# Mixture-of-experts lists summed in SBUF by matmuls of one-hot place parts, instead of records scattered to memory

## The chip, the cores and the metric

The kernel runs on one core of a Trainium2 chip. The metric is device time in microseconds for one execution, the median of several runs. The profile is of one execution; its times are in microseconds from the start of the span. Engines: PE is the matrix engine (PEld its weight loads), DVE the vector engine, ACT the scalar engine, POOL the GpSimd engine, SP the engine whose queue issues most transfers.

## The reference

Clustered attention on 4 batches x 8 heads x 768 tokens x 64 dimensions, followed by a top-2 mixture of experts on its output (3072 tokens, 512 wide, 8 experts with 1024 hidden units):

```python
mask = q_assign[:, :, :, None] == k_assign[:, :, None, :]   # nearest of 16 centroids
attn = softmax(where(mask, scale * q @ k.T, -1e9)) @ v
...
noisy_logits = x @ w_gate + log1p(exp(x @ w_noise)) * noise
top2 = np.argpartition(-noisy_logits, 2, axis=1)[:, :2]
...
for e in range(E):
    for k in range(2):
        mask = top2[:, k] == e
        h = np.maximum(x[mask] @ w1[e], 0.0)
        out[mask] += top2_w[mask, k, None] * (h @ w2[e])
```

So each token belongs to two experts, with two weights. An expert works on the list of its tokens, and the lists depend on the data.

## The kernel before

**Attention** runs over 16 pairs of heads (four pairs to a batch), 12 steps to a pair, 192 steps in all, in an order of instructions that is fixed by hand: the table `AT` gives for each piece of work the step (in thirds) at which it is issued, and each engine runs its instructions in the order of issue. A step t issues, in this order: the pieces placed at t; `scores(t)` (L477: four matmuls on PE, two exponentials on ACT); `split_p(t - 1)` (L489: the low half `pl` of the exponentials, one subtraction on POOL, L495); pieces placed at t + 1/3; `values(t - 4)` (L498: 18 small matmuls on PE, of which the last six read `pl`, L518); pieces placed at t + 2/3. So PE may run some four steps ahead of POOL. The pieces placed are the preparation of later pairs (transposes and similarities to centroids, `a_...`, the row maxima `b_max`, L446, two matmuls and two reductions on DVE), the values' scaling (`v_...`), and, for each finished batch, the gate.

**The gate** of batch b (`g_logits`, `g_turn`, `g_gate`) works out for 768 tokens the two experts, the two weights, and each token's place in its expert's list: `places` counts by matmuls with a triangle and with ones, `self.base` carries the counts on from batch to batch. A place is a whole number 4096 e + n; its low 7 bits are the partition, the bits above it the tile of 128 places and the expert. Small operations on DVE work in the PSUM tile `aux`, which also holds half of the maxima of `b_max`.

**The lists** are in memory: `tbl` has for each partition, expert and tile a record (token, weight), cleared in `zero_list` to the token number N, which transfers pass over. `g_list` (L697) is called 12 times for each batch, one step apart from step z + 24 on (steps 76, 124 and 172 for the first three batches); each call is a one-element memset on POOL (`spacer`, L700) and an indirect transfer that POOL issues (L701), which scatters 128 records. The last batch's gate and its 12 scatters stand in the experts' stage.

**Experts.** Each expert has room for 832 tokens, six and a half tiles of 128 (T = 7); `extra` (L851) is a branch with loops for longer lists, run only where the counts ask for it. For expert 0 four tiles are taken from the first three batches only (`TA = 4`): their list `lst0` is loaded by `load_list(0)` at step 183, and `gather_x` (L923: a memset and an indirect transfer on POOL) is issued at steps 185 to 188. In `experts` (L731) the last batch's gate is cut into four parts with a block of layer 1 (12 matmuls of 512 columns, L951, then ACT L960 and DVE L961) after each; then come `count` (four small DVE operations), `g_list`, four rounds of splitting a part of w2 (L903 and L904) and a block of layer 1, `load_list(1)` (the whole list from memory), the gathers of tiles 4 to 6, and layer 2 of tiles 0 to 3, with the transposes of tiles 4 to 6 (`turn_x`, L941) ahead of tile 3's. Layer 2 is L990; DVE weighs its rows (L997, L999) and POOL scatters them into `out` (L1003). For experts 1 to 7 the rows of `out` are gathered first (L966).

## Time and profile before

| | us |
|---|---|
| median of 3 runs | 1154.22 (1153.69 to 1156.89) |
| profiled execution: its time / its span | 1154.92 / 1153.1 |
| PE busy | 1076.4 (93%) |
| DVE busy | 596.7 (52%) |
| POOL busy | 589.6 (51%) |
| ACT busy | 480.4 (42%) |
| scatters of records (L701) on POOL | 51.8 in 48 |
| granted PE clock, mean | 0.969 |

Attention ends at about 520 us of the span, and expert 0's layer 2 begins at 552. A row of the timeline is: start, duration, engine, line, operation, output <- inputs, count, and in brackets the idle time before it with what ended it. A row of the stretches is: the stretch, its length, busy time with count for PE, PEld, DVE, ACT and POOL, the granted clock, the share of the transfer engines and GB/s. A row of the groups is: line, engine, operation, shapes, count, busy us, mean ns, and the idle time before with its releasers.

### The profile page before, as it was taken

The numbers are of one execution on the slowest core, as the hardware profiler recorded it, in microseconds if no ns is written. First come the engines' busy times: TensorE is split into PE (matmuls) and PEld (weight loads), VectorE is DVE, ScalarE is ACT, GpSimd is POOL, SyncE is SP. The second block draws the span as 40 slices with busy tenths as digits, with TensorE's granted clock in tenths as the row PEclk, the third lists the DMA queues.
The fourth block names the chain that finished last, engine by engine and source line by source line (L and its number), as shares of the span: only waits on it lengthen the run. The fifth ranks groups of instructions, "written<-read, shape, count | busy, mean of one in ns | idle before, by whom it ended". The sixth has DMA issues, their size and how long they took to land. (4 is left out here: it accounts for less than half of the span.)

```text
span 1153.1 us, 22350 instructions
## 1 busy us (share of the span) xinstructions
PE 1076.4 (93%) x8658; PEld 954.6 (83%) x8658; DVE 596.7 (52%) x1286; ACT 480.4 (42%) x961; POOL 589.6 (51%) x631
## 2 busy tenths in 40 slices
PE   4899899998999899869899999999999999999995
PEld 4588887898888788757799989889898898998984
DVE  5877665876687668436235334433344244433411
ACT  3475656675777566534133303223133132231300
POOL 4776664789578958991645224332343233423311
PEclk8899999999999999969999999999999999999998
DMA  8866776664656444113326225323352244323200
GB/s 224 189 151 152 188 185 194 158 158 110 192 122 159 113 127 122 33 43 118 109 75 210 81 102 166 120 93 109 127 172 73 77 162 129 118 83 131 74 31 31
DMA packets 87678, 144.46 MB, mean 125 GB/s; under 512 B 14296, under 2 KB 65880, under 8 KB 87057
## 3 DMA queue, kind: packets, MB, share of 16 engines
q1 hardware_dynamic: 72272, 106.45, 34.7%
q0 software_dynamic: 13712, 36.42, 9.4%
q8 instruction: 69, 1.13, 0.4%
q10 hardware_dynamic: 1584, 0.13, 0.1%
q14 instruction: 41, 0.33, 0.1%
HBM read 78.21 MB, written 26.53 MB: 91 GB/s over the span
## 5 line engine op out<-in xcount | busy, mean ns | idle before, releaser
L495 POOL TENSOR_TENSOR pl<-pe 128x768 f16<-128x768 f32 x192 | 280.6, 1471 | 97.4 <-ACT pe L486 90.0
L951 PE MATMUL ring<-xT,w1t 128*128 128x416 f32 (+2 forms) x1536 | 290.3, 350 | 0.0
L951 PEld LDWEIGHTS ring<-xT,w1t 128*128 128x128 f32 x1536 | 282.7, 188 | 6.6 <-DVE xT L904 0.3
L990 PE MATMUL ring<-w2t,hT 128*128 128x512 f32 x1152 | 273.7, 394 | 0.0
L990 PEld LDWEIGHTS ring<-w2t,hT 128*128 128x128 f32 x1152 | 214.5, 189 | 43.3
L486 ACT ACTIVATE pe<-ring,l 128x384 f32<-128x384 f32 x384 | 202.9, 578 | 102.5 <-PE ring L485 93.4
L1003 POOL DMA_INDIRECT out<-yo,lst x56 | 65.6, 1172 | 234.7 <-DVE yo L999 187.1
L457 DVE TENSOR_REDUCE aux<-ring 128x1 f32<-128x384 f32 x192 | 107.9, 562 | 94.6 <-PE ring L454 90.2
L485 PE MATMUL ring<-A 128*128 128x384 f32 x384 | 145.4, 379 | 0.0
L485 PE MATMUL ring<-B 128*128 128x384 f32 x384 | 134.3, 350 | 5.0 <-DMA B<-nt 4.9
L960 ACT ACTIVATE hT<-ring 128x416 fp32r<-128x416 f32 (+3 forms) x128 | 56.7, 488 | 180.6 <-PE ring L951 180.5
L961 DVE SCALAR_TENSOR_TENSOR hT<-ring,hT 128x416 fp32r<-128x416 f32 (+3 forms) x128 | 66.2, 553 | 124.0 <-ACT hT L960 123.8
L930 POOL DMA_INDIRECT xg<-xs,lst x56 | 65.5, 1170 | 124.9 <-PE ring L941 105.0
L454 PE MATMUL ring<-A 128*128 128x384 f32 x384 | 114.0, 372 | 14.5 <-DMA A<-mk 8.6
L999 DVE SCALAR_TENSOR_TENSOR yo<-ring,lst,xt 128x512 f32<-128x512 f32 (+1 forms) x49 | 36.7, 750 | 166.6 <-PE ring L990 146.1
L903 ACT ACTIVATE xT<-ring 128x512 fp32r<-128x512 f32 (+1 forms) x56 | 31.0, 565 | 178.0 <-PE ring L941 177.9
L457 DVE TENSOR_REDUCE mm<-ring 128x1 f32<-128x384 f32 x192 | 104.9, 546 | 0.0
L512 PE MATMUL av<-vv,pe 128*128 128x65 f16 x1152 | 100.9, 198 | 0.0
L514 PE MATMUL av<-vv,pe 128*128 128x64 f16 x1152 | 99.9, 196 | 0.0
L454 PEld LDWEIGHTS ring<-A 128*128 128x128 f32 x384 | 71.6, 197 | 31.0 <-ACT pe L486 14.1
L512 PEld LDWEIGHTS <-pe 128*128 128x128 bf16 x1152 | 83.6, 101 | 13.9 <-issue 11.4
L518 PE MATMUL av<-vv,pl 128*128 128x65 f16 x1152 | 68.9, 197 | 20.1 <-POOL spacer L700 12.6
(172 smaller groups left out, 1363.1 us busy)
## 6 DMA issues: line engine op xcount, KB each, us to landing
stg<-in_moe_w SPq DMA_DIRECT2D x64, 512.0 KB
A<-hl SPq DMA_DIRECT2D x30, 384.0 KB
B<-hl SPq DMA_DIRECT2D x30, 384.0 KB
vt<-in_v SPq DMA_DIRECT2D x8, 768.0 KB
out<-zt SPq DMA_DIRECT2D x12, 512.0 KB
xs<-xt SPq DMA_DIRECT2D x4, 1536.0 KB
A<-hl SPq DMA_DIRECT2D x60, 96.0 KB
B<-hl SPq DMA_DIRECT2D x30, 192.0 KB
```

The costliest lines, as they stand in the source:

```text
L454: nc.tensor.matmul(t, A[:, 0, s, j * 128:j * 128 + 128], A[:, 1, s, n * 384:n * 384 + 384], start=True, stop=True)
L457: nc.vector.tensor_reduce(o, t, axis=X, op=OP.max, negate=True)
L485: nc.tensor.matmul(t, M[:, 1 - qi, s, ks], M[:, qi, s, ns], start=not qi, stop=bool(qi))
L486: nc.scalar.activation(pe[:, n], t, AF.Exp, bias=self.l64[:, 0:1], scale=self.scale)
L495: nc.gpsimd.tensor_tensor(lo, pe, hi, op=OP.subtract)
L512: nc.tensor.matmul(av[:, j, :], ph[:, js], vv[:, hh, kj, 64:129], start=(kc == 0 and j == 0), stop=False, skip_group_check=True)
L514: nc.tensor.matmul(av[:, j, :64], ph[:, js], vv[:, hh, kj, 0:64], start=False, stop=False, skip_group_check=True)
L518: nc.tensor.matmul(av[:, j, :], pl[:, js], vv[:, hh, kj, 64:129], start=False, stop=(kc == NJ - 1), skip_group_check=True)
L951: nc.tensor.matmul(p, self.w1t[:, wi, c, f * 128:f * 128 + 128], self.xT[:, xi, c, n0:n1], start=(i == 0), stop=(i == 3 * ND - 1))
L961: nc.vector.scalar_tensor_tensor(h1, x, 0.0, h0, op0=OP.max, op1=OP.subtract)
L990: nc.tensor.matmul(p, self.hT[:, hi, f, t * 128:t * 128 + 128], self.w2t[:, wi, f], start=(i == 0), stop=(i == 3 * NF - 1))
L1003: i = nc.gpsimd.indirect_dma_start(out=self.out, out_offset=bass.IndirectOffsetOnAxis(ap=en[:r, 0:1], axis=0), in_=yo[:r], in_offset=None, ...
```

## The change

- `zero_list` and the 48 scatters are gone from the normal course. The table is cleared and all 48 scatters are issued only inside the branch for lists of more than seven tiles (`table`).
- The gate ends in other operations: the place is cut into its low 7 bits and the rest; `hot` compares the rest of 12 places for each partition with the 56 numbers of expert and tile (one DVE operation of 672 elements, `eq`); ACT copies of the low part, of a weight and of the place are added. It needs the same small DVE operations but one.
- `g_list` is called once for each batch, at step z + 26 (steps 78, 126 and 174, and at its old place in the experts' stage). It works in two halves of six columns: DVE makes `hot` (128 x 6 x 128: the low part compared with 0 to 127), POOL makes `ent` in four products of 128 x 168 (`eq` times token number minus N, and `eq` times weight), and six fp32 matmuls of `hot` (128 x 128) and `ent` (128 x 112) add into one PSUM tile. `hot` and `ent` have one buffer each. DVE then adds the 128 x 112 sum into `lacc` in SBUF, which begins as N for the tokens and 0 for the weights.
- `load_list` copies the token numbers from `lacc` to integers on DVE, in place of the loads from memory. Weights are read from `lacc` (`lsw0` for the first four tiles of expert 0).
- Five constants more are made at the start on POOL, and the values' tile `vv` has two buffers in place of three.

```diff
-    logstep=0.667, turn=7.667, list=24.0, lstep=1.0, bstep=1.0,
+    logstep=0.667, turn=7.667, list=26.0, bstep=1.0,
...
+        self.T = -(-CAP // 128)
+        self.upper = consts.tile([128, E, self.T], F32, name="upper")
+        nc.gpsimd.iota(self.upper, pattern=[[4096, E], [128, self.T]], base=0, channel_multiplier=0,
+                       allow_small_or_imprecise_dtypes=True)
+        self.lower = consts.tile([128, 128], F32, name="lower")
+        nc.gpsimd.iota(self.lower, pattern=[[1, 128]], base=0, channel_multiplier=0,
+                       allow_small_or_imprecise_dtypes=True)
+        self.tokn = consts.tile([128, B, NJ], F32, name="tokn")
+        nc.gpsimd.iota(self.tokn, pattern=[[self.S, B], [1, NJ]], base=-self.N, channel_multiplier=NJ,
+                       allow_small_or_imprecise_dtypes=True)
+        self.lacc = consts.tile([128, 2, E * self.T], F32, name="lacc")
+        nc.gpsimd.memset(self.lacc[:, 0], float(self.N))
+        nc.gpsimd.memset(self.lacc[:, 1], 0.0)
+        self.code = consts.tile([128, B, NJ, 2], I32, name="code")
+        self.wts = consts.tile([128, B, NJ, 2], F32, name="wts")
...
-                for j in range(2 * NJ):
-                    at(z + T["list"] + T["lstep"] * j, self.g_list, b, j)
-        at(T["zero"] - 4, self.zero_list)
+                at(z + T["list"], self.g_list, b)
...
-            vv = self.wk.tile([128, 4, NJ, 130], F16, name="vv", bufs=3)
+            vv = self.wk.tile([128, 4, NJ, 130], F16, name="vv", bufs=2)
...
-        self.recs = []
...
-    def zero_list(self):
-        nc, E = self.nc, self.E
-        ti = self.gp.tile([128, self.ET, 2], I32, name="lg")
-        nc.gpsimd.memset(ti[:, :, 0:1], self.N)
-        nc.gpsimd.memset(ti[:, :, 1:2], 0)
-        W = 2 * self.ET
-        nc.sync.dma_start(rap(self.tbl, 0, [[E * W, 128], [W, E], [1, W]]),
-                          ti.rearrange("p t c -> p (t c)")[:, None, :].to_broadcast([128, E, W]))
...
-        pk = lambda i: T["pk"][:, i]
...
-        pi = lambda i: T["p"][:, 440 + 2 * NJ * i:440 + 2 * NJ * i + 2 * NJ].bitcast(I32).rearrange("p (j k) -> p j k", k=2)
+        pf = lambda i: T["p"][:, 440 + 2 * NJ * i:440 + 2 * NJ * i + 2 * NJ].rearrange("p (j k) -> p j k", k=2)
+        pi = lambda i: pf(i).bitcast(I32)
...
-        rf = lambda: T["rec"].bitcast(F32)
+        wt = lambda k: self.wts[:, b, :, k]
...
-        do(lambda: nc.gpsimd.tensor_copy(T["rec"][:, :, :, 0], self.tok[:, b, :, None].to_broadcast([128, NJ, 2])))
+        do(lambda: v.tensor_scalar(T["lo"], pi(0), 127, None, op0=OP.bitwise_and))
...
-        do(lambda: v.tensor_scalar(pi(1), pi(0), 127, 8, op0=OP.bitwise_and, op1=OP.logical_shift_left))
-        do(lambda: v.tensor_scalar(pk(0), pi(0), 7, None, op0=OP.logical_shift_right))
-        do(lambda: nc.scalar.activation(rf()[:, :, 0, 1], pm(1), AF.Copy))
-        def end():
-            v.tensor_tensor(pk(1), pi(1), pk(0), op=OP.bitwise_or)
-            v.tensor_tensor(rf()[:, :, 1, 1], pm(1), m(1), op=OP.mult)
-            self.addr, self.rec = pk(1), T["rec"]
-        do(end)
+        do(lambda: nc.scalar.activation(pf(1), T["lo"], AF.Copy))
+        do(lambda: v.tensor_tensor(pf(2), pi(0), T["lo"], op=OP.subtract))
+        do(lambda: nc.scalar.activation(wt(0), pm(1), AF.Copy))
+        do(lambda: v.tensor_tensor(wt(1), pm(1), m(1), op=OP.mult))
+        def hot():
+            n, W = 2 * NJ, E * self.T
+            T["eq"] = gp.tile([128, NJ, 2, W], F32, name="lg")
+            v.tensor_tensor(T["eq"].rearrange("p j k w -> p (j k) w"),
+                            pf(2).rearrange("p j k -> p (j k)")[:, :, None].to_broadcast([128, n, W]),
+                            self.upper.rearrange("p e t -> p (e t)")[:, None, :].to_broadcast([128, n, W]), op=OP.is_equal)
+            self.eq, self.low = T["eq"], pf(1).rearrange("p j k -> p (j k)")
+        do(hot)
+        do(lambda: nc.scalar.activation(self.code[:, b], pi(0), AF.Copy))
...
-    def g_list(self, b, i):
-        nc, tc = self.nc, self.tc
-        j, k = divmod(i, 2)
-        nc.gpsimd.memset(self.spacer, 0.0)
-        i = nc.gpsimd.indirect_dma_start(
-            out=self.tbl, out_offset=bass.IndirectOffsetOnAxis(ap=self.addr[:, j, k:k + 1], axis=0),
-            in_=self.rec[:, j, k, :], in_offset=None)
-        for o in self.recs:
-            tc.declare_no_dep(i.ins, o.ins, reason="each place is one token's")
-        self.recs.append(i)
+    def g_list(self, b):
+        nc, NJ, W = self.nc, self.NJ, self.E * self.T
+        t = self.ps()[:, :2 * W]
+        n = NJ // 2
+        for h in range(2):
+            js = slice(n * h, n * h + n)
+            hot = self.gp.tile([128, NJ, 128], F32, name="hot", bufs=1)
+            nc.vector.tensor_tensor(hot, self.low[:, NJ * h:NJ * h + NJ, None].to_broadcast([128, NJ, 128]),
+                                    self.lower[:, None, :].to_broadcast([128, NJ, 128]), op=OP.is_equal)
+            ent = self.gp.tile([128, n, 2, 2, W], F32, name="ent", bufs=1)
+            for k in range(2):
+                nc.gpsimd.tensor_tensor(ent[:, :, k, 0], self.eq[:, js, k],
+                                        self.tokn[:, b, js, None].to_broadcast([128, n, W]), op=OP.mult)
+                nc.gpsimd.tensor_tensor(ent[:, :, k, 1], self.eq[:, js, k],
+                                        self.wts[:, b, js, k, None].to_broadcast([128, n, W]), op=OP.mult)
+            ent = ent.rearrange("p j k a w -> p (j k) (a w)")
+            for i in range(NJ):
+                nc.tensor.matmul(t, hot[:, i], ent[:, i], start=(h == 0 and i == 0), stop=(h == 1 and i == NJ - 1))
+        acc = self.lacc.rearrange("p a w -> p (a w)")
+        nc.vector.tensor_tensor(acc, t, acc, op=OP.add)
+    def table(self):
+        nc, B, NJ, E = self.nc, self.B, self.NJ, self.E
+        ti = self.gp.tile([128, self.ET, 2], I32, name="lg")
+        nc.gpsimd.memset(ti[:, :, 0:1], self.N)
+        nc.gpsimd.memset(ti[:, :, 1:2], 0)
+        W = 2 * self.ET
+        nc.sync.dma_start(rap(self.tbl, 0, [[E * W, 128], [W, E], [1, W]]),
+                          ti.rearrange("p t c -> p (t c)")[:, None, :].to_broadcast([128, E, W]))
+        rec = self.gp.tile([128, B, NJ, 2, 2], I32, name="rec", bufs=1)
+        pk = self.gp.tile([128, 2, B, NJ, 2], I32, name="pk", bufs=1)
+        for k in range(2):
+            nc.gpsimd.tensor_copy(rec[:, :, :, k, 0], self.tok)
+        nc.gpsimd.tensor_copy(rec.bitcast(F32)[:, :, :, :, 1], self.wts)
+        nc.vector.tensor_scalar(pk[:, 0], self.code, 127, 8, op0=OP.bitwise_and, op1=OP.logical_shift_left)
+        nc.vector.tensor_scalar(pk[:, 1], self.code, 7, None, op0=OP.logical_shift_right)
+        nc.vector.tensor_tensor(pk[:, 0], pk[:, 0], pk[:, 1], op=OP.bitwise_or)
+        for b in range(B):
+            for j in range(NJ):
+                for k in range(2):
+                    nc.gpsimd.indirect_dma_start(
+                        out=self.tbl, out_offset=bass.IndirectOffsetOnAxis(ap=pk[:, 0, b, j, k:k + 1], axis=0),
+                        in_=rec[:, b, j, k, :], in_offset=None)
...
-        self.lst0 = self.mw.tile([128, self.TA, 2], I32, name="lst0")
+        self.lst0 = self.mw.tile([128, self.TA], I32, name="lst0")
+        self.lsw0 = self.mw.tile([128, self.TA], F32, name="lsw0")
...
-        W = 2 * self.ET
+        nc, TA = self.nc, self.TA
...
-            assert len(self.recs) == 2 * self.NJ * (self.B - 1)
-            self.nc.sync.dma_start(self.lst0.rearrange("p t c -> p (t c)"), rap(self.tbl, 0, [[self.E * W, 128], [1, 2 * self.TA]]))
+            nc.vector.tensor_copy(self.lst0, self.lacc[:, 0, 0:TA])
+            nc.vector.tensor_copy(self.lsw0, self.lacc[:, 1, 0:TA])
...
-            self.nc.sync.dma_start(self.lst.rearrange("p e t c -> p e (t c)"),
-                                   rap(self.tbl, 0, [[self.E * W, 128], [W, self.E], [1, 2 * self.T]]))
+            nc.vector.tensor_copy(self.lst, self.lacc[:, 0])
...
-        return self.lst0[:, t] if e == 0 and t < self.TA else self.lst[:, e, t]
+        if e == 0 and t < self.TA:
+            return self.lst0[:, t:t + 1]
+        i = e * self.T + t
+        return self.lst[:, i:i + 1]
+    def weight(self, e, t):
+        if e == 0 and t < self.TA:
+            return self.lsw0[:, t:t + 1]
+        i = e * self.T + t
+        return self.lacc[:, 1, i:i + 1]
...
-        for i in range(2 * NJ):
-            self.g_list(b, i)
+        self.g_list(b)
...
+            self.table()
...
-            in_offset=bass.IndirectOffsetOnAxis(ap=self.entry(e, t)[:r, 0:1], axis=0),
+            in_offset=bass.IndirectOffsetOnAxis(ap=self.entry(e, t)[:r], axis=0),
...

```

More of the change, by code (lines that the diff above doesn't have):

```diff
@@ L604, in begin @@
             T["m"] = gp.tile([128, 3, NJ], F32, name="gm", bufs=1)
-            T["rec"] = gp.tile([128, NJ, 2, 2], I32, name="rec", bufs=2)
-            T["pk"] = gp.tile([128, 2, NJ, 2], I32, name="pk", bufs=2)
+            T["lo"] = gp.tile([128, NJ, 2], I32, name="glo", bufs=1)
             T["tmp"] = gp.tile([128, NJ, 2, E], F32, name="gtmp", bufs=1)
@@ L739, in experts @@
         self.w2t = mo.tile([128, 2, NF, DM], F32R, name="w2t")
-        self.lst = mo.tile([128, E, T, 2], I32, name="lst")
+        self.lst = mo.tile([128, E * T], I32, name="lst")
         A = (0, TA * 128)
@@ L967, in gather_out @@
             out=self.pv[t % 6][:r], out_offset=None, in_=self.out,
-            in_offset=bass.IndirectOffsetOnAxis(ap=self.entry(e, t)[:r, 0:1], axis=0),
+            in_offset=bass.IndirectOffsetOnAxis(ap=self.entry(e, t)[:r], axis=0),
             bounds_check=self.N - 1, oob_is_err=False)
@@ L994, in layer2 @@
         en = self.entry(e, t)
-        wt = en.bitcast(F32)[:r, 1:2]
+        wt = self.weight(e, t)[:r]
         if e == 0:
@@ L1003, in layer2 @@
         i = nc.gpsimd.indirect_dma_start(
-            out=self.out, out_offset=bass.IndirectOffsetOnAxis(ap=en[:r, 0:1], axis=0),
+            out=self.out, out_offset=bass.IndirectOffsetOnAxis(ap=en[:r], axis=0),
             in_=yo[:r], in_offset=None, bounds_check=self.N - 1, oob_is_err=False)
@@ L1014, in run @@
         self.CAP, self.TA = CAP, 4
-        self.T = -(-CAP // 128)
         self.CT = CAP // 128 * 128
```

## Prediction

> **What bounds the kernel now.** I read the page first, then the waits of the matrix engine (PE), then the table of stretches, then the timelines of POOL, PE and DVE around the record scatters. From the page:
>
> ```profile
> span 1153.1 us, 22350 instructions
> ...
> PE 1076.4 (93%) x8658; PEld 954.6 (83%) x8658; DVE 596.7 (52%) x1286; ACT 480.4 (42%) x961; POOL 589.6 (51%) x631
> ```
>
> PE is busy for 93% of the span, so matmuls added are paid in full unless they fall into PE's idle time, and each PE wait removed is a gain. The longest total PE waits (waited-for, us in total, times, longest):
>
> ```profile
> PE av L518 <- POOL spacer L700: 12.6, 7, 2.8
> ...
> PE av L518 <- POOL pl L495: 7.3, 7, 2.2
> ...
> PE ring L941 <- DMA xg<-xs,lst: 3.1, 1, 3.1
> ```
>
> The first is what the change can remove: PE waits for `pl`, which stands on POOL behind a scatter (L700 is the spacer ahead of it). The POOL timeline (start, duration) shows how, and rows that later parts use:
>
> ```profile
> 29.28 0.89 POOL L342 TENSOR_TENSOR vv<-vt,vv 128x384 f16<-128x384 f32 x1 [16.04 <-ACT vv L341]
> ...
> 461.67 1.47 POOL L495 TENSOR_TENSOR pl<-pe 128x768 f16<-128x768 f32 x1 [0.23 <-ACT pe L486]
> ...
> 465.10 0.09 POOL L700 MEMSET spacer<- 1x1 f32 x1
> 465.36 1.02 POOL L701 DMA_INDIRECT tbl<-rec,pk  x1 [0.16 <-POOL spacer L700]
> 466.40 1.48 POOL L495 TENSOR_TENSOR pl<-pe 128x768 f16<-128x768 f32 x1
> 467.81 0.09 POOL L700 MEMSET spacer<- 1x1 f32 x1
> ...
> 501.07 0.54 POOL L929 MEMSET xg<- 128x512 f32 x1
> ...
> 504.39 0.53 POOL L929 MEMSET xg<- 128x512 f32 x1
> ...
> 513.01 7.16 POOL L495 TENSOR_TENSOR pl<-pe 128x768 f16<-128x768 f32 x5
> ...
> 543.57 1.02 POOL L701 DMA_INDIRECT tbl<-rec,pk  x1 [23.22 <-issue]
> ...
> 566.33 1.05 POOL L930 DMA_INDIRECT xg<-xs,lst  x1 [5.54 <-DMA lst<-tbl]
> ```
>
> With a scatter in it a step costs POOL 467.81 - 465.10 = 2.71 us; without, `pl` alone runs at (7.16 - 1.47)/4 = 1.42. Stretches of 10 us (PE busy, PEld, DVE, ACT, POOL, granted clock) show what that does to PE at the end of the scatters of batches 0, 1 and 2:
>
> ```profile
> 260.00:270.00 10.00, 6.95 (x95) 6.22 (x92) 6.53 (x16) 3.66 (x8) 9.42 (x12) 0.97 0.78 185
> 270.00:280.00 10.00, 10.00 (x111) 9.28 (x112) 5.59 (x12) 7.15 (x14) 9.97 (x8) 0.86 0.21 54
> ...
> 380.00:390.00 10.00, 6.87 (x77) 5.89 (x76) 4.53 (x11) 3.73 (x7) 9.61 (x10) 0.83 0.47 124
> ...
> 490.00:500.00 10.00, 5.74 (x71) 4.99 (x72) 6.49 (x6) 4.08 (x7) 9.42 (x11) 0.74 0.06 20
> 500.00:510.00 10.00, 8.29 (x78) 7.39 (x76) 3.25 (x5) 5.17 (x9) 9.11 (x10) 0.67 0.20 54
> ```
>
> POOL is full in all of them, PE is not, and the granted clock falls after each gap. In batches 0 and 1 PE's head start (`values` runs four steps behind `scores`) swallows most of the scatters.
>
> **What goes, batches 0 to 2.** Batch 0 loses 10 - 6.95 = 3.05 us idle and 0.14 x 10 = 1.4 us of clock: 4.5. Batch 1 loses 3.13 + 0.17 x 6.87 = 4.3. In batch 2 POOL sets the pace to the end of attention at 513.01 + 7.16 = 520.2; that is worked out below.
>
> **What each new list costs in attention.** `g_list` is now one block at the head of a step, ahead of that step's scores in PE's order. It has two halves in single buffers: on POOL four products of 128 x 168 (`ent`), on DVE one 128 x 768 comparison (`hot`), on PE six fp32 matmuls of 112 columns; the second half's `ent` and `hot` must wait until PE has read the first. On DVE the next reductions wait behind `hot`, on POOL the next `pl`, on PE everything. Prices, from the groups (busy, mean ns) and from PE's timeline:
>
> ```profile
> L951 PE MATMUL ring<-xT,w1t 128*128 128x416 f32 (+2 forms) x1536 | 290.3, 350 | 0.0
> ...
> L495 POOL TENSOR_TENSOR pl<-pe 128x768 f16<-128x768 f32 x192 | 280.6, 1471 | 97.4 <-ACT pe L486 90.0 <-PE av L518 3.2 <-DMA A<-mk 3.2
> ...
> L342 POOL TENSOR_TENSOR vv<-vt,vv 128x384 f16<-128x384 f32 x32 | 28.6, 892 | 35.1 <-ACT vv L341 35.1
> ...
> L388 PE MATMUL ring<-csum,sm 128*128 128x64 f32 x192 | 26.0, 274 | 1.6 <-ACT sm L378 1.6
> ...
> L311 DVE TENSOR_REDUCE vm<-vt 128x2 bf16<-128x768 f32 x16 | 14.8, 936 | 0.0
> ...
> L682 POOL COPY rec<-tok 128x12 int32<-128x12 int32 x4 | 0.8, 194 | 0.0
> ```
>
> ```profile
> 235.55 0.78 PE L388 MATMUL ring<-csum,sm 128*128 128x64 f32 x6
> ...
> 459.78 0.42 PE L485 MATMUL ring<-A 128*128 128x384 f32 x1
> ...
> 464.88 0.42 PE L485 MATMUL ring<-A 128*128 128x384 f32 x1
> ...
> 468.15 0.43 PE L485 MATMUL ring<-A 128*128 128x384 f32 x1
> ...
> 525.29 0.66 PE L566 MATMUL ring<-ident,xt 128*128 128x128 f32 x4
> 525.87 0.43 PE L576 MATMUL ring<-gxT,wgn 128*32 128x128 f32 x8
> ```
>
> POOL: (1471 - 892)/384 = 1.5 ns an element over a fixed 313 ns gives 0.57 us for 168 elements, 0.52 in a chain (`pl` runs 1.42 apart at 1.47 each): 2.1 us for four. Bounds: four copies of 0.19 (0.8 us) and four of 0.89 (3.6 us).
>
> The Trainium skill ("GPSIMD Engine Reference", sections 3.1 and 4.1) gives 4497 ns for a two-input product of 2048 elements, 2.2 ns each, and sends elementwise work to VectorE. By it an `ent` product would be an estimated 0.37 us, and the sum below about 4 us lower.
>
> PE: an fp32 product leaves two records (L388: 16 pairs x 2 x 3 matmuls in the code, 192 records). Six records of 64 columns take 0.78 with the last one's 0.27, so 0.10 apart; single-record transposes of 128 columns lie 0.58/4 = 0.145 apart. A list has 24 records of 112 columns. Bounds: 0.10 if columns cost nothing (2.4 us), 0.18 if they cost in proportion (4.3). I take 0.125, between the two rows: 3.0 us, 1.5 a half.
>
> DVE: `hot` about 0.95 and the comparison with the tile numbers (`eq`, 672 elements) about 0.85, by L311; each is shorter than the 2.1 us that POOL takes, so in attention POOL's half decides.
>
> Does POOL stand ahead? Scores that start at 459.78 have their `pl` done at 461.67 + 1.47 = 463.14, 3.4 us later; PE steps are (464.88 - 459.78)/3 = 1.70 apart, so PE comes to a list just as the `pl` of two steps before ends, and waits for the whole first `ent`. A list then costs PE 2.2 + 1.5 + 2.3 (second `ent` after the first matmuls, 0.2 for the handing over) + 1.5 = 7.5 us. For the clock I add 1.0, somewhat under the 1.4 that batch 0 loses after one such gap (bounds: 0, and 3.3 as in 500 to 510): 8.5.
>
> The Trainium skill ("TensorE: Matmul & The Clock Gate", Part 1) lets the clock fall only after about 3.4 us of idleness, so gaps of 2.3 us would cost no clock and the sum would be about 3 us lower; the trace differs, with 0.86 granted in 270 to 280 although no PE wait behind a spacer is longer than 2.8.
>
> Batch 0: 8.5 - 4.5 = **+4.0**. Batch 1: 8.5 - 4.3 = **+4.2**. Batch 2: the first scatter (465.36) is step 172's, whose scores start at 464.88; those of step 174, where the new list stands, start at 468.15. PE leaves the list at 476.7; four steps still have `b_max` (1.70 each, to 483.5), seven do not and go at POOL's 1.42 (493.5); `pl` follows a step later, so the first gather of `xg` starts at about 495 in place of 501.1. From there POOL's work is as before (520.2 - 501.1 = 19.1, gathers at 504.39 - 501.07 = 3.3 a step), so attention ends at 514.1: **-6.1**.
>
> **The last batch, in the experts' stage.** PE and DVE timelines:
>
> ```profile
> 538.28 13.90 PE L951 MATMUL ring<-xT,w1t 128*128 128x512 f32 x60
> ...
> 571.57 1.70 PE L941 MATMUL ring<-ident,xg 128*128 128x128 f32 x12 [3.08 <-DMA xg<-xs,lst]
> 573.20 7.30 PE L990 MATMUL ring<-w2t,hT 128*128 128x512 f32 x24
> ...
> 595.65 5.74 PE L990 MATMUL ring<-w2t,hT 128*128 128x512 f32 x24
> ```
>
> ```profile
> 542.69 0.16 DVE L691 TENSOR_TENSOR rec<-aux,gm 128x6 f32<-128x6 f32 x1
> 543.09 0.69 DVE L961 SCALAR_TENSOR_TENSOR hT<-ring,hT 128x512 fp32r<-128x512 f32 x1 [0.24 <-ACT hT L960]
> ...
> 544.34 1.23 DVE L904 TENSOR_TENSOR w2t<-stg,w2t 128x1024 fp32r<-128x1024 f32 x1
> ```
>
> Now the twelve scatters (from 543.57 on), the list's way back from memory and the gather at 566.33 run under layer 1 and layer 2, and only 3.08 us of PE idle plus 7.30 - 5.74 = 1.6 of slow clock come out: 4.6 gained. But the list's matmuls stand in PE's order after the fourth of eight layer-1 blocks, which is done at 538.28 + 12 x 13.90/60 = 541.1. They need `hot`: the gate chain ends near 542.7 as before (one small DVE operation fewer, two more copies of 0.2 on ACT beside them), `eq` to 543.6, the fourth block's L961 and the count's four (543.09 to 544.34: 1.25), then `hot`: 545.9; POOL's first `ent` is ready then too. PE waits 4.9, then 1.5 + 2.3 + 1.5, plus 1.0 of clock: 11.2. Net **+6.6**. The gather for tiles 4 to 6 is early by then, and copies replace the list's two loads on SP's queue; behind them stood loads of weights, and the list of waits has no wait of PE on those.
>
> Edits at nothing: five more constants on POOL at the start lie before its 16.04 us idle ahead of 29.28; the clearing of the table goes from SP's queue, where it held up nothing that PE waited for; `vv` in two buffers is first written at step 24g - 18 and its old contents last read at 24g - 21, both from the schedule; the table's code under the branch for long lists is not run (L951 has 8 x 8 x 24 = 1536 records, none of an extra tile). If a cover failed, the constants would cost about 1 us, and `vv` up to a step (1.7 us) for each of six groups.
>
> **Sum.** 4.0 + 4.2 - 6.1 + 6.6 = +8.7 on the profiled run's 1154.9 (span 1153.1), 1163.6; that run lies 0.7 over the median, so 1163. All costs at their low ends (a list at 4.3) give about -7, all at their high ends over +30.
>
> **Rivals.**
> 1. Faster: relief of POOL wins, because its first `ent` is ready when PE comes and the halves are cheap. For: POOL is over 90% busy in the five stretches; against: L342 and L495 fix POOL's price. With a list at x, attention gives 3x - 23.4 (2.1 at x = 8.5), so beside +6.6 for the last batch the sum changes sign at x = 5.6. At a first wait of 0.9, halves and second wait of 1.3 and no clock, x is 4.8 and the last batch 4.9 + 3.9 - 4.6 = +4.2: -4.8 in all, 1149.
> 2. The list's wait takes hold of DVE: the second `hot` and the sum into `lacc` hold up its reductions while PE waits, and DVE, with 3 us of new work, is late for PE afterwards. 3 us a batch more in attention: 1172. Against: DVE is busy only 6.5 of 10 in 260 to 270.
> 3. The change does not do what it says in batch 2: with the scatters gone the weight splits and gathers hold the pace at what it was, and -6.1 is 0: 1169.
>
> **How the numbers follow.** Forecast 0.60, rival 1 0.20, rival 2 0.12, rival 3 0.08. The forecast's own range is 1157 to 1169; the range of 8 in 10 takes in rival 1's and rival 2's times: 1148 to 1173. Beyond 0.3% (3.5 us, about what a measurement of this kernel tells from none): slower 0.71, the same 0.09, faster 0.20, the forecast's low tail going to "the same".
>
> **What would show it.** PE idle of about 2 us before each half's matmuls, released by `ent` on POOL; POOL no longer full in 355 to 390; attention over some 6 us earlier after batch 2's list than before, less what batches 0 and 1 lost; a wait of 4 to 5 us after the fourth layer-1 block; no wait on `xg`. It is wrong if PE finds `ent` ready, if a list's records are under 0.08 or over 0.2 apart, or if the last batch's list costs PE less than 7 us.

## The result and the profile after

The changed kernel takes 1168.1 us (median of 5 runs, 1166.29 to 1168.73), the kernel before 1153.9 in the same comparison (5 runs): ratio 1.0109, 95% interval 1.0093 to 1.0125. It is slower by 1.1%. The profiled execution took 1168.35 us, 13.5 us more of span than before. From the page of the changed kernel:

```profile
span 1166.6 us, 22515 instructions
...
PE 1096.1 (94%) x8754; PEld 972.0 (83%) x8754; DVE 606.2 (52%) x1301; ACT 480.1 (41%) x969; POOL 549.2 (47%) x566
```

POOL lost 40 us of work (589.6 before) and PE gained 20. The lists' matmuls are 21.4, by the groups of the changed kernel:

```profile
L724 PE MATMUL ring<-ent,hot 128*128 128x112 f32 x96 | 21.4, 390 | 17.0 <-DVE hot L714 10.4 <-POOL ent L720 6.4
L714 DVE TENSOR_TENSOR hot<-aux,lower 128x768 f32<-128x768 f32 x8 | 7.6, 953 | 9.6 <-PE ring L724 9.6
L718 POOL TENSOR_TENSOR ent<-lg,tokn 128x168 f32<-128x168 f32 x16 | 7.5, 467 | 37.7 <-DVE lg L696 24.6 <-PE ring L724 13.0
```

The waits of PE (waited-for, us in total, times, longest) show a new one at the top, in two rows, 16.8 us together. The wait behind the spacer (12.6) and the one on `xg` (3.1) are gone:

```profile
PE ring L724 <- DVE hot L714: 10.4, 3, 5.4
...
PE ring L724 <- POOL ent L720: 6.4, 6, 1.4
PE av L532 <- POOL pl L509: 5.2, 7, 2.5
```

PE's timeline of the changed kernel around the lists of batch 0, batch 2 and the last batch (a list is two groups of 12 records):

```profile
242.11 1.56 PE L724 MATMUL ring<-ent,hot 128*128 128x112 f32 x12 [2.48 <-DVE hot L714]
244.81 3.28 PE L724 MATMUL ring<-ent,hot 128*128 128x112 f32 x12 [1.14 <-POOL ent L720]
...
477.21 0.45 PE L724 MATMUL ring<-ent,hot 128*128 128x112 f32 x2 [1.45 <-POOL ent L720]
478.00 1.37 PE L724 MATMUL ring<-ent,hot 128*128 128x112 f32 x10 [0.35 <-POOL ent L720]
480.51 3.29 PE L724 MATMUL ring<-ent,hot 128*128 128x112 f32 x12 [1.14 <-POOL ent L720]
...
541.98 3.04 PE L1004 MATMUL ring<-xT,w1t 128*128 128x512 f32 x12
550.43 2.87 PE L724 MATMUL ring<-ent,hot 128*128 128x112 f32 x12 [5.41 <-DVE hot L714]
554.44 3.28 PE L724 MATMUL ring<-ent,hot 128*128 128x112 f32 x12 [1.14 <-POOL ent L720]
557.40 13.16 PE L1004 MATMUL ring<-xT,w1t 128*128 128x512 f32 x48
...
588.09 5.75 PE L1043 MATMUL ring<-w2t,hT 128*128 128x512 f32 x24
```

The same 12 records take 1.56 us in one half and 2.87 to 3.29 in others. The reason is the granted clock, which is 0.50 in the four stretches below (same columns as before), one at each list:

```profile
243.73:250.56 6.83, 5.68 (x25) 5.14 (x26) 2.10 (x5) 1.16 (x2) 3.71 (x7) 0.50 0.00 2
363.20:370.02 6.82, 5.61 (x24) 5.10 (x24) 1.32 (x3) 0.08 (x1) 3.24 (x6) 0.50 0.06 21
479.25:486.08 6.83, 5.62 (x30) 4.95 (x29) 1.85 (x4) 1.16 (x2) 3.45 (x6) 0.50 0.00 0
547.52:561.17 13.65, 9.54 (x33) 8.29 (x34) 4.45 (x9) 1.49 (x3) 3.41 (x8) 0.50 0.05 14
```

Half of PE's busy time there is an estimate of what the low clock cost it: 2.8 us in each of batches 0 to 2 and 4.8 in the last.

Where the 13.5 us arose, by places that both timelines have (start of a step's scores, end of the last `pl`, start of layer 1 for the remaining tiles of expert 0):

| place | before | after | difference | of which new |
|---|---|---|---|---|
| scores of step 76 | 236.71 | 235.49 | -1.2 | -1.2 |
| scores of step 172 | 464.88 | 471.84 | +7.0 | lists of batches 0 and 1: +8.2 |
| end of attention | 520.17 | 522.81 | +2.6 | batch 2: -4.3 |
| layer 1, remaining tiles | 580.34 | 593.68 | +13.3 | last batch: +10.7 |

The -1.2 lies ahead of the first list and is one execution against one; its cause was not followed up. Behind expert 0 two more differences all but cancel: experts 1 to 7 take 521.2 us (625.60 to 1146.77) where the kernel before takes 518.1 (612.29 to 1130.34), with the same 2593 matmul records and PE busy throughout, and the end behind them is 3.0 us shorter. Their causes are open.

### The profile page after: what moved, and what is told of

Same layout as the page of the kernel before. It is cut to its first block, busy times and chain, and to the rows that moved or that the text cites. A ratio compares the mean times of both kernels' runs of the same rounds, so it can differ in the third digit from the quotient of the medians.

```text
span 1166.6 us, 22515 instructions
## 1 busy us (share of the span) xinstructions
PE 1096.1 (94%) x8754; PEld 972.0 (83%) x8754; DVE 606.2 (52%) x1301; ACT 480.1 (41%) x969; POOL 549.2 (47%) x566
## 3 DMA queue, kind: packets, MB, share of 16 engines
q8 instruction: 70, 1.15, 0.4%
## 5 line engine op out<-in xcount | busy, mean ns | idle before, releaser
L1004 PE MATMUL ring<-xT,w1t 128*128 128x416 f32 (+2 forms) x1536 | 295.7, 353 | 0.0
L1004 PEld LDWEIGHTS ring<-xT,w1t 128*128 128x128 f32 x1536 | 285.7, 189 | 8.7 <-DVE xT L957 0.2
L1052 DVE SCALAR_TENSOR_TENSOR yo<-ring,lacc,xt 128x512 f32<-128x512 f32 (+1 forms) x49 | 36.7, 750 | 167.2 <-PE ring L1043 146.3
L468 PEld LDWEIGHTS ring<-A 128*128 128x128 f32 x384 | 72.4, 199 | 29.2 <-ACT pe L500 13.7
L526 PEld LDWEIGHTS <-pe 128*128 128x128 bf16 x1152 | 81.7, 100 | 15.3 <-issue 11.3
L528 PEld LDWEIGHTS <-pe 128*128 128x128 bf16 x1152 | 79.5, 99 | 0.3
```

Of the source, the lines that this page charges most:

```text
L468: nc.tensor.matmul(t, A[:, 0, s, j * 128:j * 128 + 128], A[:, 1, s, n * 384:n * 384 + 384], start=True, stop=True)
L526: nc.tensor.matmul(av[:, j, :], ph[:, js], vv[:, hh, kj, 64:129], start=(kc == 0 and j == 0), stop=False, skip_group_check=True)
L528: nc.tensor.matmul(av[:, j, :64], ph[:, js], vv[:, hh, kj, 0:64], start=False, stop=False, skip_group_check=True)
L1004: nc.tensor.matmul(p, self.w1t[:, wi, c, f * 128:f * 128 + 128], self.xT[:, xi, c, n0:n1], start=(i == 0), stop=(i == 3 * ND - 1))
```

## The experiments

### Who waits for whom: the halves taken apart

The theory after this reading: the work of a list is cheap, and the loss is that its pieces stand in one block, so that PE waits at the block's head for DVE and POOL, and the clock falls. The first three kernels cut `g_list` in two functions for each half, `l_make` (`hot` on DVE, `ent` on POOL) and `l_add` (six matmuls, and the sum into `lacc`), and place them apart, with the same operations: in attention, in the last batch, and in both.

```diff
-                at(z + T["list"], self.g_list, b)
+                at(z + 25, self.l_make, b, 0)
+                at(z + 26, self.l_add, b, 0)
+                at(z + 27, self.l_make, b, 1)
+                at(z + 28, self.l_add, b, 1)
```

> The changed kernel (1168.1), with each list of batches 0 to 2 cut into four pieces that are issued a step apart: half 0 is made on DVE and POOL at z + 25, multiplied and added into lacc at z + 26, half 1 made at z + 27, multiplied and added at z + 28. PE then finds each half ready. Theory 'waits and clock': in the changed kernel batch 0's list costs PE 2.48 + 1.14 of waiting, 1.7 us because its second half runs at a low clock (3.28 against 1.56 for the first) and some 1.2 us of low clock after it; 5 to 6.6 us go in each of batches 0 and 1, and about 4 in batch 2, where POOL soon sets the pace: 1168 - 16 = 1152 (1149 to 1156), and L724's two halves at 1.5 us each with no wait in front. Rival 'work': the new instructions themselves are what costs, wherever they stand: 1165 to 1169.

Measured: 1152.42 us, ratio 0.9959 (0.9938 to 0.9979). The groups of this kernel (L751 is attention, L727 the unchanged block of the last batch):

```profile
L751 PE MATMUL ring<-ent,hot 128*128 128x112 f32 x72 | 10.6, 303 | 3.5 <-DVE hot L736 3.5
...
L727 PE MATMUL ring<-ent,hot 128*128 128x112 f32 x24 | 6.1, 435 | 6.6 <-DVE hot L717 5.4 <-POOL ent L723 1.1
```

PE's waits for three lists fall from 10.5 to 3.5 us, and the end of attention moves from 522.8 to 505.7. Of these 17.1 us, 2.8 lie ahead of the first list (the scores of step 76 start at 232.73 in place of 235.49); the rest is still twice the 7 us of waits.

```diff
-        self.g_list(b)
+        self.l_make(b, 0)
         for i in range(4):
...
                 self.layer1(0, f, [A])
                 f += 1
+            if i == 1:
+                self.l_add(b, 0)
+                self.l_make(b, 1)
+            if i == 3:
+                self.l_add(b, 1)
```

> The changed kernel (1168.1), with only the last batch's list moved: half 0 is made where the list stood, its matmuls stand after two more blocks of layer 1, half 1 is made then and its matmuls stand after the eighth block. Theory 'waits and clock': the waits of 5.41 and 1.14, the low clock of both halves (1.3 + 1.7) and of the layer 1 blocks after them (1.9) go: 11 us, 1157 (1155 to 1160). Rival 'work': 1166 to 1169. Rival 'late list': the gathers of tiles 4 to 6 are now too late for the transposes and a wait on them comes back: 1160 or more, with a PE wait on xg.

Measured: 1157.66 us, ratio 1.0011 (0.9994 to 1.0028). PE's timeline there:

```profile
549.50 1.54 PE L748 MATMUL ring<-ent,hot 128*128 128x112 f32 x12
...
556.49 1.49 PE L748 MATMUL ring<-ent,hot 128*128 128x112 f32 x12
```

No wait and full clock: the last batch's block alone was 0.98% of the time, 11 us, and without it only 3.0 us of matmuls are left of that list.

> The changed kernel with both of these moves. If the two costs are separate and add, 1168 - 16 - 11 = 1141 (1137 to 1146), under the kernel before (1153.9); under rival 'work' 1163 or more.

Measured, with both edits: 1141.38 us, ratio 0.9865 (0.9839 to 0.9891). The two gains add, and the changed kernel's own operations, issued apart, are 1.3% faster than the kernel before.

### Clock or waits: the gaps filled

PE runs matmuls that nobody reads (512 columns, in rounded fp32) ahead of each half, 7 and 4 in attention, 22 and 4 in the last batch, so that it isn't idle while it waits for `hot`. The block stays as it is.

```diff
+            if FILLS[b == self.B - 1][h]:
+                t2 = self.ps()
+                for i in range(FILLS[b == self.B - 1][h]):
+                    nc.tensor.matmul(t2, self.wh[:, 0, :128], ...[:, 512 * (i % 3):512 * (i % 3) + 512], ...)
             for i in range(NJ):
                 nc.tensor.matmul(t, hot[:, i], ent[:, i], ...)
```

> The changed kernel as it stands, but ahead of each half's matmuls PE runs matmuls that need nothing and that nobody reads (512 columns, about 0.23 us each): 7 and 4 in attention, 22 and 4 in the last batch, a little less than the waits of 2.5, 1.1, 5.4 and 1.1 us. The waits remain, PE is merely not idle in them. Theory 'clock': the granted clock stays up, the second half takes 1.5 in place of 3.2, the first half of the last batch 1.5 in place of 2.9, and the work after each list runs at full speed: 2.7 us each in batches 0 and 1, 2 in batch 2, 5 in the last: 1156 (1153 to 1160). If the clock is not what makes the second half slow (contention on its operands, say), 1168 to 1171 and the second half stays at 3.2.

Measured: 1158.74 us, ratio 1.0016 (1.0001 to 1.0031). PE's timeline for batch 0:

```profile
238.18 1.86 PE L729 MATMUL ring<-wh 128*128 128x512 f32 x7
240.82 1.56 PE L732 MATMUL ring<-ent,hot 128*128 128x112 f32 x12 [0.77 <-DVE hot L717]
242.15 1.17 PE L729 MATMUL ring<-wh 128*128 128x512 f32 x4
243.52 0.45 PE L732 MATMUL ring<-ent,hot 128*128 128x112 f32 x2 [0.20 <-POOL ent L723]
244.34 1.37 PE L732 MATMUL ring<-ent,hot 128*128 128x112 f32 x10 [0.37 <-POOL ent L723]
```

The list's matmuls still start when `hot` and `ent` are there, but the second half now takes 0.45 + 0.37 + 1.37 = 2.2 us in place of 3.3, and the kernel is 0.93% faster than the changed one (1.0016 against 1.0109), some 10.7 us, for matmuls that compute nothing. Around all four lists the granted clock is now 1.00. So the clock alone makes up most of the change's net loss of 1.1%. Of the whole price of the block, 2.4% by the kernel with both edits (1.0109 to 0.9865), it is some two fifths. The idle PE in the wait is what brings the clock down.

### The price of the matmuls

The six matmuls of each half run twice, the first time into a PSUM tile that nothing reads.

```diff
+            for i in range(NJ):
+                nc.tensor.matmul(t2, hot[:, i], ent[:, i], start=(h == 0 and i == 0), stop=(h == 1 and i == NJ - 1))
             for i in range(NJ):
                 nc.tensor.matmul(t, hot[:, i], ent[:, i], start=(h == 0 and i == 0), stop=(h == 1 and i == NJ - 1))
```

> The changed kernel (1168.1 beside a kernel before of 1153.9), each half's six matmuls run twice, the first time into a PSUM tile that nobody reads. Everything else waits as before, and the second half's operands wait for both rounds of the first. If the matmuls count in full where PE waits for them: 1.4 us at full clock for the first half, 1.4 to 3.0 for the second, so some 4 us in each of batches 0, 1 and the last, and 0 to 4 in batch 2: +11 to +17 over the changed kernel, a ratio to before of 1.022 to 1.028. Rival 'hidden': the list costs only its waits, and matmuls in them are free: +0 to +3, a ratio of 1.011 to 1.015.

Measured: 1183.03 us, ratio 1.0224 (1.0204 to 1.0245), 1.15% over the changed kernel: 13.3 us for 96 more records, 0.14 each. That is the price between the two clocks. PE's timeline of this kernel for batch 0 (L726 the round that isn't read, L728 the one that is):

```profile
242.59 1.92 PE L726 MATMUL ring<-ent,hot 128*128 128x112 f32 x12 [2.50 <-DVE hot L714]
244.30 2.77 PE L728 MATMUL ring<-ent,hot 128*128 128x112 f32 x12
```

The second round waits for nothing and stands right behind the first; it takes 2.77 us where 1.56 would do. A matmul in the path is paid in full here, as the prediction took it.

### The values' tile with two buffers

The kernel before with `vv` in two buffers in place of three, and nothing else.

> The kernel before with one edit of the change alone: the values' tile vv in two buffers in place of three. The prediction put this at nothing, and at up to 1.7 us for each of six groups (10 us, ratio 1.009) if its old contents were read later than the schedule says. Theory: ratio 0.999 to 1.001. Rival (the buffer takes part in the change's loss): 1.004 to 1.009.

Measured: 1154.41 us against 1157.66 of the kernel before beside it, ratio 0.9987 (0.9962 to 1.0012). This part of the change costs nothing that can be measured.

### What POOL's relief is worth

The spaced kernel (both edits above), with 36 scatters put back on POOL in attention, twelve for each batch, one step apart behind a spacer as before; they write a table that nothing reads.

```diff
+                for j in range(2 * NJ):
+                    at(z + 24 + j, self.idle_scatter, b, j)
```

> The kernel with both moves (1141.4 beside 1156.5), and on POOL in attention the old scatters again: for each of batches 0 to 2 twelve memsets and twelve indirect transfers of 128 records, one a step from z + 24 on, to rows of the table that nothing reads (the records are not the lists'; the lists come from SBUF). Measures what the removed scatters cost by themselves. By the prediction's terms: 4.5 in batch 0, 4.3 in batch 1, and in batch 2, where POOL sets the pace, 12 x 1.27 = 15 us: +19 to +24 over the kernel with both moves, a ratio to before of 1.003 to 1.008. Rival 'little relief': +0 to +6, a ratio of 0.987 to 0.992.

Measured: 1166.8 us, ratio 1.0096 (1.0074 to 1.0118). The last five `pl` of attention on POOL, first in the spaced kernel and then with the scatters:

```profile
499.12 7.15 POOL L512 TENSOR_TENSOR pl<-pe 128x768 f16<-128x768 f32 x5
```

```profile
518.28 7.16 POOL L517 TENSOR_TENSOR pl<-pe 128x768 f16<-128x768 f32 x5
```

Attention ends 19.2 us later. Of this, 1.4 lie ahead of the first scatter (scores of step 76: 234.56 against 233.12), 4.8 arise in batches 0 and 1 (up to the scores of step 172: 466.94 against 460.70), and 12.9 in batch 2. So the scatters cost 17.7 us here, and in the first two batches about half of what the prediction had for the kernel before (4.5 + 4.3). The whole time grew by 2.3%, some 26.7 us, of which the profiled runs show 25.5. The 6.3 us behind attention stay open: at 612 us the difference of the two is still 19.2, experts 1 to 7 then take 2.3 us more and the end behind them 4.1, where neither edit stands. What the relief is worth in the changed kernel was not measured by itself; attention ended later there, so the lists' block took more than it.

### Made earlier, and in rounded fp32

With `l_make` of the first half at z + 24, a step earlier:

```diff
-                at(z + 25, self.l_make, b, 0)
+                at(z + 24, self.l_make, b, 0)
```

> The kernel with both moves, with half 0 of batches 0 to 2 made at z + 24 in place of z + 25, two steps ahead of its matmuls. In the kernel with both moves PE still waits 1.5, 1.5 and 0.5 us for hot. If that wait goes: 3 us less, a ratio to before of 0.984 (0.982 to 0.986). If DVE is what is late, and hot in an earlier place only pushes the reductions behind it: no difference, 0.9865.

Measured: 1138.24 us, ratio 0.9848 (0.9829 to 0.9867). By its groups PE waits for no list any more, and a record costs 279 ns with its latency where the changed kernel had 390:

```profile
L751 PE MATMUL ring<-ent,hot 128*128 128x112 f32 x96 | 12.4, 279 | 0.0
```

The next three have `hot` and `ent` in rounded fp32, which leaves one record for a matmul where fp32 leaves two; a weight then goes in as a rounded part and the rest of it, so `ent` has 168 columns.

```diff
-        ent = self.gp.tile([128, n, 2, 2, W], F32, name="ent", bufs=1)
+        ent = self.gp.tile([128, n, 2, 3, W], F32R, name="ent", bufs=1)
...
+            nc.scalar.activation(self.wh2[:, 0], self.wts[:, b], AF.Copy)
+            nc.vector.tensor_tensor(self.wh2[:, 1], self.wts[:, b], self.wh2[:, 0], op=OP.subtract)
         for k in range(2):
+            nc.gpsimd.tensor_tensor(ent[:, :, k, 2], self.eq[:, js, k],
+                                    self.wh2[:, 1, js, k, None].to_broadcast([128, n, W]), op=OP.mult)
```

> As e8_early_make, with hot and ent in the rounded fp32 type of the other matmuls (one record for each matmul, where fp32 leaves two), the weights as two parts, so 168 columns in place of 112 and two more products on POOL for each half. A half's twelve records of 0.117 us (1.5 us) become six of about 0.1 (0.7 us): 1.6 us less a list where PE is the bound (batches 0, 1 and the last), 5 us in all against e8: a ratio to before of 0.980 (0.977 to 0.983). If matmul time is not what is left of a list's cost, or POOL's additional products show, no less than e8.

Measured: 1141.92 us, ratio 0.9876 (0.9852 to 0.9900), a miss. The matmuls are cheaper, but PE waits again, by the list of waits of this kernel, now that POOL makes six products for a half in place of four:

```profile
PE ring L757 <- POOL ent L748: 13.9, 14, 3.1
```

Next the products with the rest of the weight move from POOL to DVE, into a tile of their own:

```diff
-            nc.gpsimd.tensor_tensor(ent[:, :, k, 2], self.eq[:, js, k],
+            nc.vector.tensor_tensor(ent[:, :, k, 2], self.eq[:, js, k],
```

> As e9_rounded (hot and ent in rounded fp32, one record for a matmul, weights as a high and a low part), but the products with the low part are made on DVE, so POOL makes four products of a half as in e8_early_make, and the two parts have a tile of their own. Theory (e9's miss was POOL's two more products and the late split): PE no longer waits for ent, a half takes about 0.95 us in place of 1.55, 8 x 0.6 = 4.8 us less than e8: ratio 0.980 to 0.982. Rival (rounded matmuls give nothing whatever makes ent, because the lists' matmuls are hidden by POOL's pace in attention): only the last batch's halves count, 1.2 us, 0.983 to 0.985. If the wait on ent stays, 0.987 as in e9.

Measured: 1141.81 us, ratio 0.9871 (0.9827 to 0.9916), a miss too, and its cause lies in DVE's and POOL's timelines of batch 0 and of the second half:

```profile
237.29 3.02 DVE L742 TENSOR_TENSOR ent<-lg,wh 128x168 fp32r<-128x168 f32 x2
...
246.47 0.57 DVE L742 TENSOR_TENSOR ent<-lg,wh 128x168 fp32r<-128x168 f32 x2
```

```profile
235.72 2.90 POOL L510 TENSOR_TENSOR pl<-pe 128x768 f16<-128x768 f32 x2
238.55 0.14 POOL L343 MEMSET vv<- 128x48 f16 x1
238.65 1.49 POOL L510 TENSOR_TENSOR pl<-pe 128x768 f16<-128x768 f32 x1
```

DVE's two products take 3.02 us where the next two take 0.57: the first (1.51 us) ends 0.2 us after POOL's second `pl` does (238.62), the second 0.2 us after the third (240.14). PE waits 2.95 us, by the list of waits for a reduction that stands behind them on DVE, and its clock falls (0.56 in 240 to 241, 0.50 in 241 to 242). The last kernel joins DVE's two products into one and gives the pieces more steps:

```diff
+        nc.vector.tensor_tensor(ent[:, :, :, 2], self.eq[:, js],
+                                self.wh2[:, 1, js, :, None].to_broadcast([128, n, 2, W]), op=OP.mult)
...
-                at(z + 26, self.l_add, b, 0)
-                at(z + 27, self.l_make, b, 1)
-                at(z + 28, self.l_add, b, 1)
+                at(z + 27, self.l_add, b, 0)
+                at(z + 28, self.l_make, b, 1)
+                at(z + 31, self.l_add, b, 1)
```

> As e10_rounded_dve, with the two products that DVE makes for a half joined into one, and with more steps between the pieces in attention: made at z + 24, added at z + 27, made at z + 28, added at z + 31. In e10 PE still waited 2.95 us in batch 0 because DVE's two products, 0.32 us each elsewhere, took 1.51 and 1.59 beside POOL's pl; one product can meet at most one pl (1.5). Theory: no PE wait before a half, halves of 0.95 in place of e8's 1.55, ratio 0.980 to 0.982. Rival (in attention the halves' shorter matmuls give nothing, since POOL or DVE paces it): 0.984 to 0.986, like e8.

Measured: 1136.08 us, ratio 0.9822 (0.9805 to 0.9838). Of all versions it has the lowest time, 1.8% under the kernel before and 2.8% under the changed one (0.9822 / 1.0109 = 0.972). By its groups the lists' matmuls wait for 0.4 us only and are down to 8.7 us of PE:

```profile
L755 PE MATMUL ring<-ent,hot 128*128 128x168 f32 x48 | 8.7, 330 | 0.4 <-DVE ent L741 0.4
```

But this is not why it is fast. The wait has moved: `hot` and DVE's product, made early, stand ahead of the row maxima on DVE, and the scores of a later step wait for those in batches 0 and 1:

```profile
PE ring L500 <- DVE aux L472: 3.1, 2, 1.5
```

The clock falls in batches 0, 1 and 2 again (0.50 in 241.78 to 245.20, 357.84 to 361.25 and 470.48 to 473.89). From the scores of step 76 to layer 1 of expert 1 this kernel takes 366.3 us (234.04 to 600.37), the one with fp32 made a step earlier 359.4 (235.06 to 594.42). The gain lies in experts 1 to 7, where no list is made. From layer 1 of expert 1 to the last full tile of layer 2, first the kernel made earlier and then this one:

```profile
594.42:1115.59 521.17, 521.17 (x2593) 468.02 (x2592) 198.72 (x318) 133.94 (x262) 170.15 (x234) 1.00 0.34 113
```

```profile
600.37:1114.64 514.27, 514.27 (x2593) 462.73 (x2592) 198.74 (x318) 134.03 (x262) 169.28 (x234) 1.00 0.35 114
```

The same number of matmuls takes 6.9 us less, with PE busy throughout in both. All three rounded kernels show it (513.1, 514.3, 514.3), and all three reach expert 1 later than the fp32 one (608.51, 605.64, 600.37 against 594.42). Why the experts are shorter was not tried. The three also hold `upper` and `lower` in bfloat16 and put the tiles of the branch for long lists into the buffers of `hot` and `ent`, and no run has that alone. So nothing here shows that rounded matmuls make a list cheaper as a whole.

## Why the prediction was right or wrong

The direction was right, and the time (1168.1) lies in the range, close to the upper end of the forecast's own 1157 to 1169. The profiled run rose by 13.5 where the sum said 8.7: 8.2 - 4.3 + 10.7, less the 1.2 ahead of the first list, where the prediction has 8.2 - 6.1 + 6.6.

**Batches 0 and 1: +4.0 and +4.2 predicted, +8.2 measured for both**, but by terms whose errors offset, so that the agreement is in part luck. With the predicted loss of the scatters (8.8 for the two) a list cost (8.2 + 8.8) / 2 = 8.5, the predicted figure. By PE's own timeline it cost more, 2.48 + 1.14 of waiting, 3.0 of matmuls at full clock and 2.8 of clock in batch 0, 9.4 in all, and the scatters put back into the spaced kernel cost 4.8 for the two and not 8.8. How the 8.2 divides between list and relief stays open. Inside the list:
- *The first wait, "2.2 for the first `ent`"*: 2.48 in batch 0, but for `hot`. The step that failed is "each is shorter than the 2.1 us that POOL takes, so in attention POOL's half decides". It compared durations and left out DVE's queue. POOL had its four products by 240.55; DVE was in its reductions until 241.0:

```profile
240.48 0.55 DVE L471 TENSOR_REDUCE mm<-ring 128x1 f32<-128x384 f32 x1
...
241.01 0.95 DVE L714 TENSOR_TENSOR hot<-aux,lower 128x768 f32<-128x768 f32 x1
```

```profile
238.80 0.47 POOL L718 TENSOR_TENSOR ent<-lg,tokn 128x168 f32<-128x168 f32 x1
...
240.08 0.47 POOL L720 TENSOR_TENSOR ent<-lg,wts 128x168 f32<-128x168 f32 x1
```

  That PE finds `ent` ready was named as a sign against the prediction. It holds in batches 0 and 1 and in the last batch (PE waits three times for `hot`); in batch 2 `ent` was later (1.45).
- *The second wait, "2.3"*: 1.14. The four products need not all be there: the first matmul reads only the first pair, and `hot` (0.95) runs beside them. The rest of `ent` shows as 0.35 in batch 2's first half, and in the second halves as some 0.4 among the slow records (3.28, where the last batch's first half, which had all its `ent`, took 2.87).
- *The records, "0.125 apart"*: (1.56 - 0.28) / 11 = 0.117 at full clock. Right.
- *An `ent` product, "0.57, 0.52 in a chain"*: 0.47, and 0.43 in a chain (the first of four starts at 238.80, the fourth at 240.08: 1.28 / 3). The Trainium skill's figure ("GPSIMD Engine Reference", sections 3.1 and 4.1; an estimated 0.37) lay as far below as the prediction lay above.
- *The clock, "1.0, somewhat under the 1.4 that batch 0 loses"*: 2.8 in each batch. This is the term of the sum that was mis-sized. It was scaled from one gap of before, as if the loss grew with the gap. The changed kernel's stretches of 1 us show steps instead:

```profile
243.00:244.00 1.00, 0.67 (x7) 0.49 (x5) 0.29 (x1) 0.00 (x0) 0.18 (x1) 0.87 0.32 111
244.00:245.00 1.00, 0.19 (x1) 0.22 (x2) 0.67 (x1) 0.00 (x0) 1.00 (x3) 0.50 0.01 5
...
249.00:250.00 1.00, 1.00 (x6) 0.69 (x5) 0.24 (x1) 1.00 (x2) 0.00 (x0) 0.50 0.00 0
250.00:251.00 1.00, 1.00 (x23) 1.00 (x22) 0.78 (x2) 0.28 (x2) 0.91 (x1) 0.72 0.00 0
```

  The clock goes from 1.00 to 0.50 at about 243.7 and back at about 250.6, and PE has work for 5.68 us of that time. What a fall costs depends on how long it lasts and how busy PE is in it: before, batch 0's fall lasted 3.4 us (269.43 to 272.85), here it is 6.8 in batches 0 to 2 and 13.7 in the last.

**Batch 2: -6.1 predicted, -4.3 measured.** The way was as told: POOL sets the pace, so what counts is when the gathers start. With step 172 later by 7.0, 495 becomes 502.0; measured 503.38, by POOL's timeline:

```profile
503.38 0.52 POOL L982 MEMSET xg<- 128x512 f32 x1
...
515.66 7.15 POOL L509 TENSOR_TENSOR pl<-pe 128x768 f16<-128x768 f32 x5
```

From there it is 19.4 to the end of attention (19.1 predicted). PE left the list at 480.51 + 3.29 = 483.8, where the prediction, moved by 7.0, has 483.7. But the clock stayed at 0.50 until 486.0, which costs the steps behind the list 1.1 of the 1.4: the clock's term again.

**The last batch: +6.6 predicted, +10.7 measured.** The wait for `hot` was 5.41 (4.9 predicted), for the reason given: `eq` and the small operations stand ahead of it on DVE. The gains came as told: no wait on `xg`, and the tile after it at 5.75 in place of 7.30. What failed is again "plus 1.0 of clock": the list from 550.43 to 557.40 took 6.97 with its waits where 1.5 + 2.3 + 1.5 was predicted, the 48 matmuls of layer 1 behind it 13.16 where before's rate gives 48 x 13.90/60 = 11.1. And from the end of attention to the end of the fourth block 1.3 more went by than before (19.17 + 3.04 against 18.11 + 2.78), with a granted clock of 0.90 in 525 to 535 in place of 1.00. 0.5 + 1.7 + 2.0 + 1.3 - 1.0 = 4.5, against 4.1 missing; the 1.0 taken off is the predicted clock.

**Edits at nothing.** `vv` was, by its own run. The constants and the cleared table were not tried apart. The prediction has no term for experts 1 to 7 and the end behind them, where +3.1 and -3.0 us arose; that the two cancel is luck.

**The rivals.** *Rival 1* did not come about in the changed kernel. Its relation, with a list at x, is that attention gives 3x - 23.4. Counted from the scores of step 76 to the end of attention, so that what lies ahead of the first list is left out, the kernel before takes 283.5 us, the changed one 287.3, the one spaced in attention 273.0 and the one made earlier 268.9. That gives x = 9.1, 4.3 and 2.9: the first near the 9.4 of PE's timeline, the last about what the matmuls alone take (12.4 / 4 = 3.1), and both spaced ones under the 5.6 at which the sum changes sign. The 23.4 is the prediction's own figure and was not measured as such. The relief of POOL wins once the halves are apart. *Rival 2* named the right engine (DVE's `hot`), but its 3 us a batch on top did not come: batches 0 and 1 stand at the forecast's +8.2. Its mechanism, reductions that come late behind the list's work on DVE, shows in the last rounded kernel (3.1 us). *Rival 3* is out: batch 2 gained.

The Trainium skill's rule that the clock falls after about 3.4 us of idleness ("TensorE: Matmul & The Clock Gate", Part 1) is not borne out as a limit on a single gap: it fell after 2.48 us of idle in batch 0, and in batch 2 with no single gap over 1.45. Nor had PE been idle for the whole of the 3.4 us ahead of these falls: it was busy for 1.56 of them (240.32 to 243.73) and for 1.69 (475.84 to 479.25). Had the sum gone by it, it would have been 3 us lower and further off.

## What to carry to other kernels

When several engines make what one matmul group reads, place the making some steps ahead of the matmuls in the order of issue, in separate pieces: by the prediction's relation the same operations cost 9.1 us a list as a block and 2.9 to 4.3 when spaced. Price a new PE gap as wait plus a possible fall of the clock (2.8 us in attention here), not as the wait alone; if it can't be avoided, matmuls that nobody reads were worth 0.9% here. And when asking which engine is late, look at the queue that the operation joins, not at its duration. Before a lower time is put down to an edit, compare the stages that the edit doesn't touch: here they differ by 2 to 8 us from kernel to kernel, as much as the last edits were meant to bring.

## What the runs showed of the hardware

**The clock has two levels, and falls on a grid of its own.** In the stretches of 1 us it is 1.00 or 0.50. In the changed kernel it falls at 243.73, 363.20, 479.25 and 547.52, which are 35, 34 and 20 times 3.413 us apart, and it stays low for 6.83, 6.82, 6.83 and 13.65, 2 and 4 times the same. The falls come 4.1, 3.5 and 2.5 us after PE went idle in batch 0, batch 2 and the last batch (239.63, 475.76 and 545.02). So what counts, by these rows, is not the length of a gap but how idle PE is in one stretch of a grid of 3.41 us. The kernel spaced in attention shows it with one and the same wait, 1.50 us in batch 0 and 1.47 in batch 1. The stretches of its own grid (it falls at 353.74), two in batch 0 and one in batch 1:

```profile
234.28:237.69 3.41, 2.44 (x43) 1.77 (x41) 3.34 (x8) 1.24 (x3) 3.41 (x8) 1.00 0.96 229
237.69:241.10 3.41, 2.73 (x23) 2.60 (x24) 2.23 (x7) 0.70 (x2) 2.29 (x4) 1.00 0.88 319
350.33:353.74 3.41, 1.91 (x41) 1.65 (x42) 3.27 (x7) 0.38 (x1) 3.41 (x6) 1.00 0.96 303
```

In batch 0 the wait lies across two stretches, PE is idle for 1.0 and 0.7 us of them, and nothing falls; the 12 records take 1.56 us. In batch 1 it lies in one, PE is idle for 1.5, the clock is at 0.50 for the next 3.41 us, and they take 2.69. The limit is not sharp: in the kernel with the matmuls run twice, 1.8 us of idleness in one stretch (557.66 to 561.07) passed without a fall. What exactly is counted was not measured.

**DVE and POOL block each other when both of DVE's inputs are in SBUF.** `ent` on DVE (two inputs in SBUF) took 1.5 us beside `pl` on POOL and 0.32 alone, and in the kernel made earlier one POOL product took 1.33 in place of 0.47, while DVE split a part of w2 (532.59 to 533.92 beside 532.38 to 533.60). The Trainium skill ("SBUF — State Buffer", "Who interferes with whom") states that such a DVE instruction and a POOL instruction that reads SBUF exclude each other for their whole length; the trace agrees: DVE's two products end 0.2 us after a `pl` does, at 238.80 and 240.31 against 238.62 and 240.14. `hot`, with one input in PSUM, took 0.95 throughout.
